# Moving evacuations between ScalarE and VectorE, and two weight gathers behind a gate, in the opening of a fused FNet-mixing and channel-mix kernel

## The chip, the cores and the metric

The kernel runs on one core of one Trainium2 chip. The metric is the device time of one execution in microseconds, the median over several runs. The core has TensorE (PE, matrix products into PSUM), VectorE (DVE), ScalarE (ACT) and GpSimd (POOL), each with its own instruction queue that is worked off in order, and 16 DMA engines. SyncE (SP) issues DMAs only.

## The reference

The input x has 8 batches of 3072 positions by 256 features. First it is mixed by a Fourier transform over both axes, of which the real part is kept; then a channel-mix layer follows, with a shift by one position:

```python
X = np.fft.fft(x, axis=1)
X = np.fft.fft(X, axis=2)
x = X.real
x_prev = np.concatenate([np.zeros((B, 1, D)), x[:, :-1, :]], axis=1)
xk = mu_k * x + (1.0 - mu_k) * x_prev
xr = mu_r * x + (1.0 - mu_r) * x_prev
k = np.maximum(xk @ w_k, 0.0)            # w_k: 256 x 1024
v = k * k @ w_v                          # w_v: 1024 x 256
r = 1.0 / (1.0 + np.exp(-(xr @ w_r)))    # w_r: 256 x 256, "receptance"
out = r * v
```

## The kernel before

**The stages of one batch.** x is loaded and folded with its mirror image by VectorE (`fold`, L171 and L173). A first set of products (`a_sum`, L583, or `a_item` and `a_half`) with a table of sines gives `a`; a second (`d_units`, L605) gives `g_all`; `turned` (L628) puts one column in another order; a third (`c_sums`, L647) gives the mixed sequence `y` as 27 slots of 128 columns per half. From `y`, VectorE forms the difference of neighbouring slots (`diff`, L700), scales it by mu (L712) and adds it (L723), which gives the two operands x for `w_k` and `w_r`. The channel mix works on 48 chunks of 512 positions: products with `w_k` (`k_products`, L758), Relu on ScalarE (L779), square on VectorE or ScalarE (`square`, L789 and L787), products with `w_v` (`v_part`, L822, in the first chunks, `v_tile`, L810, later), products with `w_r` and a sigmoid (`r_item`, L796 and L801), and the product of both (`v_out`, L832), which is stored.

**How the order is set.** Each chunk has four steps; a table of (step, function) pairs written out by hand tells what else is issued in each step: the transforms of later batches, their loads, the mixing. At the end `pin_order` chains all the instructions of an engine in the order in which they were written, so the source order is the order of every queue. The first batch has no earlier work to hide behind. It runs in an opening stretch of some 23 us, written out line by line (L844 to L969), in which TensorE also gets matmuls on zeros (`keep_busy`, L206) that compute nothing.

**PSUM.** Products go to three slots of 128x1024 (`ps_w`) and two of 128x512 (`ps_v`), each used in turn; a product has to wait until the slot's former content has been copied out. The copy out is `evac` (L518): by VectorE if its last argument is "V", otherwise by ScalarE. Two engines that use the same PSUM tile are put one after the other.

**The angles.** The table `m_cs` for the third set of products is the sine of `ang`, an integer tile with two planes (c = 0 and 1) of 14 columns of 64. The first 6 columns come from VectorE (`m_angles`, L411), the other 8 from ScalarE (`m_angles_2`, L405), one operation of 128x512 out of PSUM for each plane. VectorE then masks them to one turn (`wrap_angles`, L402; 128x768 for the first 6 columns, 128x1024 for the other 8), and ScalarE takes the sines (`m_sine`, L442).

**The loads of the weights.** GpSimd issues them in `loads` (L452): two gathers of rows of `w_k`, a memset, the load of all of `w_v` into `wv_sb` (L456), two gathers of rows of `w_r` (L457 and L458), and then `half_rows` (L492), an iota and a comparison that make the table `order`, which TensorE uses in `half_tables` (L497, step 3). A gather is issued at L140. `w_r`'s first reader is `r_item` in step 5 (L977).

**The gate.** GpSimd's queue runs ahead of the others. To hold a load back, `load_gate` (L464) has VectorE write a 1x1 tile and GpSimd write it after that; the loads behind it in GpSimd's queue thus start no earlier than VectorE comes to that point:

```python
def load_gate():
    V.memset(gate, 0)
    iota(gate, pattern=[[0, 1]], base=0, channel_multiplier=0)
```

Its first use is `loads_1` in step 1 (L974), ahead of the loads of the second batch.

**The end of the opening** (L892 to L922). The slots 0 to 4 of `y` are in the tile `first`, 5 to 8 in `w`, 9 to 16 in the two small tiles `odd` (9, 11, 13, 15) and `even` (10, 12, 14, 16). L905 makes the first four slots of x straight from `first`. Then `y` is evacuated: 5 to 8 by ScalarE (L919), slot 4, 128x128, by ScalarE (L920), the odd ones, 128x512, by VectorE and the even ones by ScalarE (L921 and L922). After that come the first products with `w_k` (`k_early`, L961), the difference of slots 4 to 8 (L962) and the rest of the steps.

Of the kernel before, what the change touches and what calls it, by code (L numbers as in the profile page):

```python
# [13 lines left out]
AF = mybir.ActivationFunctionType  # L14
# [6 lines left out]
def _v(ap, extra_offset, free_dims):  # L21
    new_ap = [list(ap.ap[0])] + [[s, c] for (s, c) in free_dims]
    return dataclasses.replace(ap, offset=ap.offset + extra_offset, ap=new_ap)
# [16 lines left out]
def kernel(  # L40
# [10 lines left out]
    nc = tc.nc  # L51

    B, S, D = x.shape
# [24 lines left out]
    def ps_w():  # L78
        return ps_slot("W", 3, 1024)

    def ps_v():
        return ps_slot("V", 2, 512)
# [23 lines left out]
    V = nc.vector  # L106
# [32 lines left out]
    def gather(dst, src, idx):  # L139
        nc.gpsimd.indirect_dma_start(dst, None, src, bass.IndirectOffsetOnAxis(ap=idx, axis=0))  # L140
# [47 lines left out]
    wr_sb = [[const.tile([P, 256], FP16, name=f"wr{m}{a}") for a in range(2)] for m in range(2)]  # L188
# [10 lines left out]
    TURN = 1 << 22  # L199
# [50 lines left out]
    row_i = const.tile([P, 4], UINT32)  # L250
# [24 lines left out]
    def ts(out, in0, s1, op0, s2=None, op1=None):  # L275
        kw = {} if op1 is None else {"op1": op1}
        V.tensor_scalar(out=out, in0=in0, scalar1=s1, scalar2=s2, op0=op0, **kw)

    MUL, ADD = ALU.mult, ALU.add
# [47 lines left out]
    for i in range(2):  # L327
        nc.scalar.activation(out=unit[:, i:i + 1], in_=g_i[0:2], func=AF.Copy, bias=1.0 - i,
                             scale=2.0 * i - 1.0)
# [19 lines left out]
    def row(n, k=1):  # L349
# [11 lines left out]
    ph_c = const.tile([P, 4], FP32)  # L361
    ang = (k2_pool.tile([P, 8, 512], FP16, name="rl", tag="rl")
           .rearrange("p a b -> p (a b)").bitcast(INT32)[:, 0:2 * NJ * 64]
           .rearrange("p (c s t) -> p c s t", c=2, t=64))
# [20 lines left out]
    for c in range(2):  # L385
        nc.scalar.activation(out=tv(TO, 32 * c, (64, 2), (1, 32)),
                             in_=_v(one, 32 * c, [(64, 2), (1, 32)]), func=AF.Copy,
                             bias=32.0 - 64.0 * c)
# [6 lines left out]
    for g in range(2):  # L395
        kw = dict(func=AF.Sin, bias=sc[:, 2 + g:3 + g], scale=sc[:, g:g + 1])
        nc.scalar.activation(out=_v(w_pm, g, [(WA + WB, 2), (2, 2), (4, NU)]),
                             in_=_v(u_w, 0, [(0, 2), (NU, 2), (1, NU)]), **kw)
        nc.scalar.activation(out=_v(w_pm, WA + g, [(WA + WB, 2), (2, NU)]),
                             in_=_v(u_w, 2 * NU, [(0, 2), (1, NU)]), **kw)  # L400
# [2 lines left out]
        ts(ang[:, :, j0:j1], ang[:, :, j0:j1], TURN - 1, ALU.bitwise_and)  # L403

    def m_angles_2(ps, j0, j1):  # L405
        for c in range(2):
            nc.scalar.activation(out=ang[:, c, j0:j1], in_=ps[:, 0:64 * (j1 - j0)],
                                 func=AF.Identity, bias=ph_c[:, 2 * c:2 * c + 1],
                                 scale=float(TURN) / S)

    def m_angles(ps, j0, j1, z=0):  # L411
        for c in range(2):
# [36 lines left out]
    def m_first():  # L449
        nc.gpsimd.memset(_v(m_cs[hi64], 0, [(NJ * 64, 2)]), 0.0)  # L450

    def loads():  # L452
        for a in range(2):
            gather(wk_sb[0][a], moe_w_k, row_i[:, a:a + 1])
        m_first()
        nc.gpsimd.dma_start(out=wv_sb, in_=moe_w_v.rearrange("(fc p) v -> p fc v", p=128))  # L456
        for a in range(2):  # L457
            gather(wr_sb[0][a], moe_w_r, row_i[:, a:a + 1])  # L458
        half_rows()


# [2 lines left out]
    def load_gate():  # L464
        V.memset(gate, 0)  # L465
        iota(gate, pattern=[[0, 1]], base=0, channel_multiplier=0)  # L466

    def loads_1():
        load_gate()
        load_xh(1, 0)  # L470
# [21 lines left out]
    def half_rows():  # L492
        iota(order_i, pattern=[[1, 2], [2, 64]], base=0, channel_multiplier=-1)
        nc.gpsimd.tensor_scalar(out=order, in0=order_i, scalar1=0.0, scalar2=None,
                                op0=ALU.is_equal)
# [22 lines left out]
    def evac(out_ap, in_ap, eng):  # L518
        if eng == "V":
            V.tensor_copy(out=out_ap, in_=in_ap)  # L520
        else:
            nc.scalar.activation(out=out_ap, in_=in_ap, func=AF.Copy)  # L522
# [86 lines left out]
    def d_evac(ps, u0, n, bank, eng):  # L609
        evac(_v(g_all, 256 * u0, [(64, 2), (128, 2 * n), (1, 64)]),  # L610
             _v(ps, 0, [(bank, 2), (64, 2 * n), (1, 64)]), eng)
# [47 lines left out]
    def y_evac(b, s0, n, ps):  # L659
        o = s0 % 2  # L660
        evac(y_t[b][:, s0:s0 + n].rearrange("p s a t -> p (s a t)"),
             _v(ps, 512 * o, [(128, n // 2), (512 - 1024 * o, 2), (1, 128)]), "A")
# [180 lines left out]

    mu_rows()  # L844
    m_angles_2(ang_ps[1], NJ1, NJ)
    wrap_angles(NJ1, NJ)
    ts(w_pm[:, 0:2, WA:WA + WB], w_pm[:, 0:2, WA:WA + WB], math.sqrt(0.5), MUL)
# [16 lines left out]
    a_sum(0, 0, 4)  # L864
    V.tensor_copy(out=muf_t, in_=mu_ps[:, 0:6])
    loads()
    keep_busy(NF[2], ang_ps[1])
    fold(0, 1, 0, 4)
# [16 lines left out]
    w, first = ps_w(), ps_w()  # L885
# [8 lines left out]
    turned(2, 4, small[1][:, 256:258], "V")  # L894
    d_evac(fill[:, 256:1024], 4, 1, 512, "A")
    d_evac(fill[:, 384:1024], 5, 1, 512, "V")
    x_t[0, 0, 0] = mix_pool.tile([P, 2, 1536], FP16, name="x00")
    for a in range(2):
        t = x_t["t", a] = mix_pool.tile([P, 24, 64], FP16, name=f"t{a}")
        nc.scalar.activation(out=t[:, 0:4],  # L900
                             in_=_v(first, 64 * a, [(128, 2), (512, 2), (1, 64)]), func=AF.Copy,
                             scale=mu_n[:, a, 0:1])
# [7 lines left out]
    y, odd = y_t[0], ps_v()  # L910
# [6 lines left out]
    keep_busy(NF[6], w[:, 768:1024], 256)  # L917
    c_sums((even, odd), 9, 8, 1)
    y_evac(0, 5, 4, w)  # L919
    evac(y[:, 4].rearrange("p a t -> p (a t)"), first[:, 256:384], "A")  # L920
    for z, p in enumerate((odd, even)):  # L921
        evac(_v(y, 128 * (9 + z), [(256, 4), (1, 128)]), p, "VA"[z])  # L922

# [93 lines left out]
    at(21, mix, 1, 0, 0, 1, 0, 12)  # L1019
    at(22, diff, 1, 12, 26)  # L1020
    at(21, load_gate)
    at(21, load_xh, 3, 1)
    at(23, mix, 1, 0, 0, 0, 12, 24)
# [18 lines left out]
    for b in range(B):  # L1042
# [4 lines left out]
        if b and b + 3 < B:  # L1047
            at(s0 + 22, load_gate)
            for h in range(2):
                at(s0 + 22, load_xh, b + 3, h)  # L1050
        t = b + 2
        if t < B:
# [6 lines left out]
            c = [(c_pairs, t, 8 * n, (8, 8, 8, 4)[n], EV[n]) for n in range(4)]  # L1059
# [7 lines left out]
        t = b + 1  # L1067
# [67 lines left out]
```

## Time and profile before

| | us |
|---|---|
| median of 3 runs | 432.34 |
| lowest and highest run | 432.31, 433.6 |
| profiled execution, its own time | 431.6 |
| its span in the profile | 429.8 |
| TensorE busy, of the span | 422.8 |
| VectorE busy | 359.8 |
| ScalarE busy | 321.6 |
| GpSimd busy | 63.9 |

The span runs from the first to the last instruction in the trace; the profiled execution's own time has 1.8 us more around it. A row of the time line gives the start and the length in us, the engine (PEld is TensorE's load of weights), the line in the kernel, the operation, and what it writes and reads; "xN" stands for N instructions merged into one row, and the bracket tells how long the engine had been idle and what ended that. A row of the chain gives start, length and what. A row of the stretches gives the stretch, its length, busy time and number of instructions of PE, PEld, DVE, ACT and POOL, the clock granted to TensorE, the DMA share and the GB/s. "DMA to landing" counts from the start of the issue to the last byte.

### The profile page before, as it was taken

The numbers are of one execution on the slowest core, as the hardware profiler recorded it, in microseconds if no ns is written. First come the engines' busy times: TensorE is split into PE (matmuls) and PEld (weight loads), VectorE is DVE, ScalarE is ACT, GpSimd is POOL, SyncE is SP. The second block draws the span as 40 slices with busy tenths as digits, with TensorE's granted clock in tenths as the row PEclk, the third lists the DMA queues.
The fourth block names the chain that finished last, engine by engine and source line by source line (L and its number), as shares of the span: only waits on it lengthen the run. The fifth ranks groups of instructions, "written<-read, shape, count | busy, mean of one in ns | idle before, by whom it ended". The sixth has DMA issues, their size and how long they took to land.

```text
span 429.8 us, 9299 instructions
## 1 busy us (share of the span) xinstructions
PE 422.8 (98%) x3858; PEld 298.5 (69%) x3858; DVE 359.8 (84%) x545; ACT 321.6 (75%) x376; POOL 63.9 (15%) x94
## 2 busy tenths in 40 slices
PE   8999999999999999999999999999999999999996
PEld 3667776777777776776677777777767767766765
DVE  8889989997998889988898988989799847997453
ACT  8889897877878678776777777777786867666661
POOL 7568402000050002300041000500000000000000
PEclk9999999999999999999999999999999999999999
DMA  8879946322385233933258223773232322223233
GB/s 173 113 117 195 229 116 130 75 56 68 70 153 143 52 77 65 197 83 72 57 116 187 57 54 73 133 159 75 52 72 50 76 65 60 69 64 72 67 73 99
DMA packets 35102, 42.06 MB, mean 98 GB/s; under 512 B 4114, under 2 KB 31092, under 8 KB 35060
## 3 DMA queue, kind: packets, MB, share of 16 engines
q1 hardware_dynamic: 27488, 25.41, 23.9%
q0 software_dynamic: 7264, 15.80, 22.0%
q8 instruction: 30, 0.49, 0.5%
q10 hardware_dynamic: 308, 0.26, 0.2%
q14 instruction: 12, 0.10, 0.1%
HBM read 32.08 MB, written 25.17 MB: 133 GB/s over the span
## 4 chain that ended last, share of the span: by engine, by line
PE 93%; POOL 2%; DMA 2%; issue 0%; DVE 0%; ACT 0%
PE psW L758 38%; PE psV L810 36%; PE psW L796 10%; PE psV L822 3%; PE psW L605 2%; DMA wv_sb<-in_moe_w_v_dram 2%; PE psW L679 1%; PE psW L565 1%; POOL xm L140 1%; PE psW L647 1%; POOL wk L140 1%; PE psW L583 0%; ACT rl L779 0%; POOL row_i L242 0%; PE psW L542 0%
## 5 line engine op out<-in xcount | busy, mean ns | idle before, releaser
L779 ACT ACTIVATE rl<-psW 128x1024 f16<-128x1024 f32 x192 | 195.2, 1025 | 92.2 <-PE psW L758 88.6
L758 PE MATMUL psW<-x,wk 128*128 128x512 f16 (+1 forms) x776 | 195.3, 377 | 0.6 <-DVE x L723 0.4
L810 PE MATMUL psV<-wv_sb,k 128*128 128x256 f16 x1424 | 184.1, 273 | 0.0
L810 PEld LDWEIGHTS <-k 128*128 128x128 f16 x1424 | 137.0, 98 | 35.7
L789 DVE TENSOR_TENSOR k<-rl 128x2048 f16<-128x2048 f16 (+1 forms) x100 | 115.6, 1157 | 33.7 <-ACT rl L779 33.3
L758 PEld LDWEIGHTS <-wk 128*128 128x128 f16 x776 | 74.8, 98 | 53.2 <-issue 1.1
L832 DVE SCALAR_TENSOR_TENSOR o<-psV,r 128x512 f32<-128x512 f32 (+1 forms) x97 | 65.8, 681 | 14.8 <-PE psV L810 13.4
L723 DVE TENSOR_TENSOR x<-y,t 128x1536 f16<-128x1536 f16 (+3 forms) x74 | 62.1, 845 | 2.1
L796 PE MATMUL psW<-wr,x 128*128 128x256 f16 x384 | 49.8, 273 | 0.0
L801 ACT ACTIVATE r<-psW 128x1024 f16<-128x1024 f32 x48 | 48.9, 1018 | 0.8 <-PE psW L796 0.8
L796 PEld LDWEIGHTS <-x 128*128 128x128 f16 x384 | 37.5, 98 | 14.3 <-issue 0.2
L466 POOL IOTA gate<- 1x1 int32 x6 | 2.1, 356 | 202.4 <-DVE gate L465 202.4
L522 ACT ACTIVATE a<-psW 128x832 f16<-128x832 f32 x31 | 25.9, 863 | 1.4 <-PE psW L565 1.4
L522 ACT ACTIVATE g_all<-psW 128x1024 f16<-128x1024 f32 (+5 forms) x37 | 25.6, 693 | 0.4 <-PE psW L628 0.2
L140 POOL DMA_INDIRECT xm<-in_x_dram,idx_g x18 | 22.9, 1271 | 5.5 <-issue 5.2
L171 DVE TENSOR_TENSOR p<-xp,xm 112x2304 f16<-112x2304 f16 (+6 forms) x19 | 21.6, 1138 | 0.0
L712 DVE TENSOR_SCALAR t<-d,muf_t 128x1536 f16<-128x1536 f16 (+3 forms) x42 | 21.2, 518 | 0.1
L712 DVE TENSOR_SCALAR t<-d,mu_m 128x1536 f16<-128x1536 f16 x32 | 19.7, 616 | 0.0
L605 PEld LDWEIGHTS <-a 128*128 128x128 f16 x208 | 14.0, 98 | 6.8 <-ACT a L522 0.7
L182 DVE TENSOR_TENSOR eo<-p 112x1152 f16<-112x1152 f16 (+3 forms) x28 | 17.9, 679 | 0.0
L700 DVE TENSOR_TENSOR d<-y 128x1664 f16<-128x1664 f16 (+5 forms) x19 | 16.7, 881 | 0.7 <-ACT y L522 0.7
L522 ACT ACTIVATE pq<-psW 128x1024 f16<-128x1024 f32 (+1 forms) x18 | 15.2, 880 | 2.3 <-PE psW L679 2.3
(137 smaller groups left out, 219.6 us busy)
## 6 DMA issues: line engine op xcount, KB each, us to landing
out_dram<-o SPq DMA_DIRECT2D x189, 128.0 KB, 2.4
xp<-in_x_dram POOLq DMA_DIRECT2D x12, 216.0 KB, 4.5
xp<-in_x_dram POOLq DMA_DIRECT2D x13, 192.0 KB, 6.9
xp<-in_x_dram POOLq DMA_DIRECT2D x2, 384.0 KB, 6.6
wv_sb<-in_moe_w_v_dram POOLq DMA_DIRECT2D x1, 512.0 KB, 9.6
xp<-in_x_dram SPq DMA_DIRECT2D x1, 480.0 KB, 4.0
xp<-in_x_dram POOLq DMA_DIRECT2D x1, 432.0 KB, 4.8
xm<-in_x_dram,idx_g POOLq DMA_INDIRECT x18, 7.8
```

The costliest lines, as they stand in the source:

```text
L140: nc.gpsimd.indirect_dma_start(dst, None, src, bass.IndirectOffsetOnAxis(ap=idx, axis=0))
L522: nc.scalar.activation(out=out_ap, in_=in_ap, func=AF.Copy)
L605: nc.tensor.matmul(out=ps[:, o:o + 128], lhsT=a_t[b][:, e, 2 * (u0 + i):2 * (u0 + i) + 2, :], rhs=w_eo[:, e], start=True, stop=True)
L712: V.tensor_scalar(out=dst, in0=src, scalar1=mu, scalar2=None, op0=ALU.mult)
L723: V.tensor_tensor(out=_v(x_t[b, j, m], o, [(64 * step, hi - lo), (step, 64)]), in0=y_t[b][:, lo + 3 * m:hi + 3 * m, a], in1=x_t["t", a][:, ...
L758: nc.tensor.matmul(out=st["k", ds][:, 512 * hs + lo:512 * hs + hi], lhsT=wk_sb[m][a][:, 128 * fc:128 * fc + 128], rhs=xk[:, a, 512 * i + l ...
L779: nc.scalar.activation(out=st["rl"][:, 2 * ds:2 * ds + 2], in_=st["k", ds].rearrange("p (f t) -> p f t", f=2), func=AF.Relu, bias=0.0, sca ...
L789: V.tensor_tensor(out=k2_t[c][:, lo:hi], in0=r, in1=r, op=ALU.mult)
L796: nc.tensor.matmul(out=ps[:, 256 * tb:256 * tb + 256], lhsT=x_t[b, 1, m][:, a, 512 * i + 128 * tb: 512 * i + 128 * tb + 128], rhs=wr_sb[m] ...
L801: nc.scalar.activation(out=st["r", c], in_=ps, func=AF.Sigmoid)
L810: nc.tensor.matmul(out=st["v", tb - h][:, 256 * h:256 * h + 256], lhsT=k2_t[c][:, fc, 128 * tb:128 * tb + 128], rhs=wv_sb[:, fc], start=(f ...
L832: V.scalar_tensor_tensor(out=o.rearrange("p a b -> p (a b)")[:, 0:256 * n], in0=st["v", t0][:, 0:256 * n], scalar=16.0, in1=st["r", c][:, ...
```

## The change

Three edits, all in the opening. First, the angles of the second plane, which ScalarE made, are made by VectorE. Second, slot 4 of `y` is copied out by VectorE in place of ScalarE, and the odd slots 9 to 15 by ScalarE in place of VectorE. Third, the two gathers of `w_r` leave `loads` and come in a new function `loads_0`, behind a gate of their own, which is called just ahead of the tile x00; `half_rows` thereby moves up behind the load of `w_v`.

```diff
     def m_angles_2(ps, j0, j1):
-        for c in range(2):
-            nc.scalar.activation(out=ang[:, c, j0:j1], in_=ps[:, 0:64 * (j1 - j0)],
-                                 func=AF.Identity, bias=ph_c[:, 2 * c:2 * c + 1],
-                                 scale=float(TURN) / S)
+        nc.scalar.activation(out=ang[:, 0, j0:j1], in_=ps[:, 0:64 * (j1 - j0)],
+                             func=AF.Identity, bias=ph_c[:, 0:1], scale=float(TURN) / S)
+        ts(ang[:, 1, j0:j1], ps[:, 0:64 * (j1 - j0)], float(TURN) / S, MUL, ph_c[:, 2:3], ADD)
...
         nc.gpsimd.dma_start(out=wv_sb, in_=moe_w_v.rearrange("(fc p) v -> p fc v", p=128))
-        for a in range(2):
-            gather(wr_sb[0][a], moe_w_r, row_i[:, a:a + 1])
         half_rows()
...
+    def loads_0():
+        load_gate()
+        for a in range(2):
+            gather(wr_sb[0][a], moe_w_r, row_i[:, a:a + 1])
+
     def loads_1():
         load_gate()
...
     d_evac(fill[:, 384:1024], 5, 1, 512, "V")
+    loads_0()
     x_t[0, 0, 0] = mix_pool.tile([P, 2, 1536], FP16, name="x00")
...
     y_evac(0, 5, 4, w)
-    evac(y[:, 4].rearrange("p a t -> p (a t)"), first[:, 256:384], "A")
+    evac(y[:, 4].rearrange("p a t -> p (a t)"), first[:, 256:384], "V")
     for z, p in enumerate((odd, even)):
-        evac(_v(y, 128 * (9 + z), [(256, 4), (1, 128)]), p, "VA"[z])
+        evac(_v(y, 128 * (9 + z), [(256, 4), (1, 128)]), p, "A")
```

## The prediction, on record before the change was run

> **What bounds the kernel now.** I read the page first, then the chain that ended last, then TensorE's own rows in the stretch that the change touches.
>
> ```profile
> span 429.8 us, 9299 instructions
> ...
> PE 422.8 (98%) x3858; PEld 298.5 (69%) x3858; DVE 359.8 (84%) x545; ACT 321.6 (75%) x376; POOL 63.9 (15%) x94
> ```
>
> TensorE is busy for 422.8 of 429.8 us. Only 7.0 us of the span are not matmul, so a change to other engines can gain something only where one of those 7.0 us lies, or lose by adding to them. The chain (columns: start, length, what) says where TensorE takes over:
>
> ```profile
> 13.76 9.57 DMA wv_sb<-in_moe_w_v_dram
> 23.38 1.03 PE psV L822 x8
> ...
> 421.23 4.51 PE psV L810 x40
> ```
>
> From 23.38 to 421.23 + 4.51 = 425.74 the chain is in effect TensorE's program order, 402.4 us. Before 23.38 its last link is no engine: it is the load of wv_sb, issued at 13.76 and landed at 13.76 + 9.57 = 23.33. Now TensorE just before it:
>
> ```profile
> 20.10 1.03 PE L758 MATMUL psW<-x,wk 128*128 128x256 f16 x8 [0.44 <-DVE x L723]
> 20.97 0.28 PE L605 MATMUL psV<-w_eo,a 128*128 128x128 f16 x2
> 21.08 1.97 PE L758 MATMUL psW<-x,wk 128*128 128x512 f16 x8
> 23.38 0.81 PE L822 MATMUL psV<-wv_sb,k 128*128 128x256 f16 x6 [0.33 <-DMA wv_sb<-in_moe_w_v_dram]
> ```
>
> TensorE waits twice in this stretch: 0.44 us at 20.10 for the mixed x of VectorE, 0.33 us at 23.38 for wv_sb. The reader is to see their order. Whatever is saved at the first is paid back at the second, as long as wv_sb still lands at 23.33. So every part is judged by one question: when does the first L822 matmul start?
>
> **Part 1, the angle operation.** VectorE's rows, then ScalarE's:
>
> ```profile
> 6.08 0.54 DVE L277 TENSOR_SCALAR rl<-psV,ph_c 128x320 int32<-128x320 f32 x1
> 6.65 0.59 DVE L277 TENSOR_SCALAR rl<-rl 128x768 int32<-128x768 int32 x1
> 7.72 0.69 DVE L277 TENSOR_SCALAR rl<-rl 128x1024 int32<-128x1024 int32 x1 [0.48 <-ACT rl L407]
> ```
> ```profile
> 6.45 1.23 ACT L407 ACTIVATE rl<-psV,ph_c 128x512 int32<-128x512 f32 x2
> ```
>
> Removed: one of ScalarE's two, 1.23 / 2 = 0.61 us, so ScalarE is free near 7.07 instead of 7.68. Added on VectorE: the same operation on 128x512. It isn't in the trace; the nearest row is 128x320 at 0.54, so it lies between 0.54 and 0.54 x 512 / 320 = 0.86. I take 0.70, the middle, which is also about the 0.68 of a 128x512 copy out of PSUM (quoted below). In the changed instruction order it waits for ScalarE's half, which reads the same PSUM tile, but that ends near 7.07, before VectorE is through with the first mask at 6.65 + 0.59 = 7.24. So it runs 7.24 to 7.94 and the second mask starts there instead of at 7.72: VectorE had 0.48 us of idle time, uses it up and is 0.2 late (by the ends, 0.06 to 0.4). The folds of x stand behind it on VectorE and shift by 0.2. ScalarE, on the other side, reaches the sines and the table load up to 0.6 earlier. What becomes of both is read where they meet:
>
> ```profile
> 13.93 0.56 ACT L522 ACTIVATE a<-psV 128x416 f16<-128x416 f32 x1
> ```
> ```profile
> 14.54 0.40 PE L605 MATMUL psV<-w_eo,a 128*128 128x128 f16 x4 [0.23 <-ACT a L522]
> ```
>
> The next TensorE stage waits for the last evacuation of a. That one reads the product of the last fold, so it follows VectorE, and a ScalarE that is free sooner doesn't help it. I cost Part 1 at 0.1 us later at 14.54 (ends 0 and 0.4), hidden further on by the wait at 23.38.
>
> **Part 2, the evacuations of the sums.** VectorE, then ScalarE:
>
> ```profile
> 17.27 1.13 DVE L905 SCALAR_TENSOR_TENSOR x<-psW,muf_t,t 128x128 f16<-128x128 f32 x4 [0.33 <-ACT t L900]
> 18.32 0.68 DVE L520 CAST y<-psV 128x512 f16<-128x512 f32 x1
> 18.91 0.42 DVE L700 TENSOR_TENSOR d<-y 128x512 f16<-128x512 f16 x1
> ```
> ```profile
> 18.43 0.28 ACT L522 ACTIVATE y<-psW 128x128 f16<-128x128 f32 x1 [0.31 <-DVE x L905]
> 18.61 0.59 ACT L522 ACTIVATE y<-psV 128x512 f16<-128x512 f32 x1
> 19.09 0.60 ACT L522 ACTIVATE y<-psW 128x512 f16<-128x512 f32 x1
> 19.56 1.11 ACT L522 ACTIVATE g_all<-psV 128x512 f16<-128x512 f32 x2
> 20.95 1.02 ACT L779 ACTIVATE rl<-psW 128x1024 f16<-128x1024 f32 x1 [0.28 <-PE psW L758]
> ```
>
> VectorE gives away the 128x512 copy (it held the queue 18.91 - 18.32 = 0.59) and takes a 128x128 one; a 128x128 operation of L905 costs 1.13 / 4 = 0.28. So the difference at 18.91, the mixed x behind it and TensorE's matmuls at 20.10 come 0.59 - 0.28 = 0.3 earlier, inside the 0.44 waited there. ScalarE loses its 0.31 of waiting and the 128x128 copy, which moved its queue by 18.61 - 18.43 = 0.18, and gains a 128x512 copy at 19.09 - 18.61 = 0.48 of queue: 0.48 - 0.18 - 0.31 puts the two g_all copies where they were, or 0.1 later with the handover from TensorE. They end by 19.56 + 1.11 + 0.1 = 20.77, so the first L779 starts near 20.8 instead of 20.95. The square that L822 needs comes next on VectorE:
>
> ```profile
> 22.42 1.30 DVE L789 TENSOR_TENSOR k<-rl 128x1024 f16<-128x1024 f16 x2
> ```
>
> With VectorE 0.3 earlier and L779 ending near 21.8, it starts near 22.1 and ends after 1.30 / 2 = 0.65 at 22.8. TensorE's second half of 21.08, which reuses a PSUM slot that L779 frees, ends 0.15 to 0.3 before its 23.05. So without the wait for wv_sb, L822 could start near 22.95: about 0.45 is the most that Parts 1 and 2 can give, and with wv_sb at 23.33 they give nothing.
>
> **Part 3, the gathers of w_r behind a gate.** On GpSimd the two gathers stood between the wv_sb load and the two operations that make the order table; now those two come first, then the gate, then the gathers.
>
> ```profile
> 13.76 1.21 POOL L456 DMA_DIRECT2D wv_sb<-in_moe_w_v_dram  x1
> 15.27 0.98 POOL L140 DMA_INDIRECT wr<-in_moe_w_r_dram,row_i  x1 [0.30 <-issue]
> 16.56 0.94 POOL L140 DMA_INDIRECT wr<-in_moe_w_r_dram,row_i  x1 [0.30 <-issue]
> ```
> ```profile
> 16.53 0.42 DVE L520 CAST g_all<-psW 128x256 f16<-128x256 f32 x1
> ```
>
> The gate is one VectorE memset behind that copy, at 16.95, in the 0.33 of idle time before 17.27, so it costs VectorE nothing. GpSimd's iota waits for it, and what is queued behind that wait are the two gathers and, behind them, the next gate of before, which starts only at 23.20:
>
> ```profile
> 23.20 0.12 POOL L466 IOTA gate<- 1x1 int32 x1 [4.76 <-DVE gate L465]
> ```
>
> From that row, the memset (23.05) leads to the iota 0.15 later, and the next issue follows 0.23 behind it: the gathers issue at 16.95 + 0.15 + 0.23 = 17.3 and 17.3 + 0.98 + 0.30 = 18.6, 2.0 later than now, and GpSimd is done at 19.6, well ahead of 23.2. Nothing else moves. The load of wv_sb keeps its issue at 13.76, since nothing that precedes it on GpSimd was edited. Does it land earlier without the gathers close behind? The landing times of the two gathers, first and second (min/median/max over one and over two issues):
>
> ```profile
> DMA to landing us min/median/max: 8.4/8.4/8.4
> ```
> ```profile
> DMA to landing us min/median/max: 7.4/7.9/8.4
> ```
>
> They land at 15.27 + 8.4 = 23.67 and 16.56 + 7.4 = 23.96, that is 0.34 and 0.63 after wv_sb, in the order of issue. And the transfers end in a tail that a few engines make (last two columns: DMA share, GB/s):
>
> ```profile
> 21.00:22.00 1.00, 1.00 (x8) 0.47 (x6) 1.00 (x4) 1.00 (x2) 0.00 (x0) 1.00 0.34 46
> 22.00:23.00 1.00, 1.00 (x5) 0.29 (x3) 1.00 (x3) 1.00 (x2) 0.00 (x0) 1.00 0.22 29
> ```
>
> Two thirds of the DMA capacity lie idle while the last packets of wv_sb come in, so those few engines aren't short of bandwidth. They work off a queue in which the gathers stand behind. I read this as no gain for wv_sb; the bounds are 0 and the two gathers' whole share, 0.63, of which TensorE could use 0.45. The Trainium skill (DMA: Bandwidth & Descriptors, section "Two DMAs through the same engine are not ordered") says that descriptors of one queue of one SDMA engine start in order but are pipelined, which speaks against this part: by it the gathers behind can't hold up wv_sb's start, and only the pipelining leaves a little; the order of landing agrees.
>
> Sum: 0 for Part 1 and 2 (behind the wait for wv_sb), 0 for Part 3, against the profiled execution's 431.6 us. That lies 0.74 under the median of 432.34, so I forecast the median itself, rounded: **432.3 us**.
>
> **The rivals.**
> *A, forecast: wv_sb still lands near 23.3.* 432.3 us. The wait at 20.10 shrinks to 0.1 or 0.2 and the one at 23.38 grows by as much.
> *B, wv_sb lands earlier.* If the gathers' packets were interleaved with wv_sb's, it lands up to 0.63 sooner and L822 gains up to 0.45, less the 0.1 of Part 1: 0.35, so 432.0 us. For it: the gathers finish only 0.34 and 0.63 behind wv_sb, which is short for 256 rows on a queue. Against it: the order of landing, the idle capacity.
> *C, w_r is late (slower).* Its first reader:
>
> ```profile
> 27.69 1.04 PE L796 MATMUL psW<-wr,x 128*128 128x256 f16 x8
> ```
>
> The second gather, issued at 18.6, must land within 27.69 - 18.6 = 9.1 us. The rows show 7.4 and 8.4, but the slowest gather of the first 60 us needed 11.5:
>
> ```profile
> DMA to landing us min/median/max: 3.2/6.3/11.5
> ```
>
> At 11.5 it lands at 30.1, and TensorE, in order, stands for 2.4 us: 434.7 us. Below 9.1 it costs nothing. Against it: the queue ahead is empty by 24, and the next load is issued only at 23.4.
> *D, a GpSimd issue ahead of wv_sb stretches.* VectorE's shift of 0.2 changes what runs beside the gathers before 13.76. One issue can take twice its usual 0.98:
>
> ```profile
> 34.22 1.93 POOL L140 DMA_INDIRECT wr<-in_moe_w_r_dram,row_i  x1 [0.30 <-issue]
> ```
>
> That would put wv_sb 1.93 - 0.98 = 0.95 later: 433.3 us. The Trainium skill (SBUF — State Buffer, section "Who interferes with whom") has the mechanism: VectorE in a 2-port mode and GpSimd exclude each other from shared ports for a whole instruction. No row here proves that this is what stretched that issue.
>
> **How the numbers follow.** About 0.3%, 1.3 us, is what a measurement of this kernel can tell from no change. A 0.48, B 0.26, D 0.10: all three within it. C 0.12: mostly slower, since a stall of over 1.3 us needs a landing past 10.4 us. What no row prices: 0.04 faster. Faster 0.04, same 0.85, slower 0.11. The range takes in A, B and D, 0.84 together: from 432.3 less 0.45 and some scatter, 431.6, to 433.3.
>
> **What would show it.** Part 1: the second mask 0.1 to 0.3 later, the first evacuation of a earlier, L605 still at 14.5 to 14.7. Part 2: L700 near 18.6, the L758 group at 19.8. Part 3: the two gathers issued near 17.3 and 18.6, and L796 without a wait. The forecast itself: L822 starts at 23.3 to 23.4 and the wait for wv_sb there is 0.6 to 0.8. It is wrong if L822 starts under 23.2 (B), if wv_sb's issue is off 13.76 (D), or if L796 waits for w_r (C).

## The result, and the profile after

| | median, us | lowest to highest, us | runs |
|---|---|---|---|
| before, in the first comparison | 432.37 | 432.26 to 433.63 | 8 |
| changed, in the first comparison | 431.61 | 431.44 to 431.94 | 8 |
| before, beside e5, e6, e7 and e8 | 431.44 | 431.20 to 432.33, and one of 489.85 | 33 |
| changed, e5 | 431.65 | 431.32 to 431.98 | 11 |
| before, beside e13 to e16 | 431.43 | 431.19 to 432.31 | 33 |
| changed, e16 | 431.45 | 431.35 to 431.96 | 11 |

The first comparison gave a ratio of 0.9973 (95 % interval 0.9961 to 0.9986): faster by 0.76 us. Two later ones gave 1.0003 (0.9994 to 1.0012) and 1.0001 (0.9992 to 1.0010). The changed kernel took the same each time. What varied is the kernel before, which ran 0.7 to 0.9 us slower in the first comparison than in the later ones. So two things need an explanation: what can slow the kernel before, and why it doesn't slow the changed one.

The page of the changed kernel's profiled execution (431.82 us):

```profile
span 430.0 us, 9302 instructions
...
PE 423.8 (99%) x3858; PEld 299.0 (70%) x3858; DVE 360.3 (84%) x547; ACT 321.5 (75%) x375; POOL 62.9 (15%) x95
```

TensorE's rows at the end of the opening (L760 and L824 are L758 and L822 of before):

```profile
20.42 1.03 PE L760 MATMUL psW<-x,wk 128*128 128x256 f16 x8
21.29 0.28 PE L607 MATMUL psV<-w_eo,a 128*128 128x128 f16 x2
21.41 2.19 PE L760 MATMUL psW<-x,wk 128*128 128x512 f16 x8
23.49 1.05 PE L824 MATMUL psV<-wv_sb,k 128*128 128x256 f16 x8
```

The wait for wv_sb is gone, but TensorE reaches the products with w_v at 23.49, no sooner than the 23.38 of before. GpSimd's queue is what looks different. First the changed kernel, then the one before:

```profile
7.44 0.65 POOL L242 IOTA row_i<- 64x2 uint32 x4
...
8.50 0.93 POOL L140 DMA_INDIRECT xm<-in_x_dram,idx  x1
9.73 1.20 POOL L140 DMA_INDIRECT wk<-in_moe_w_k_dram,row_i  x1 [0.30 <-issue]
11.23 1.35 POOL L140 DMA_INDIRECT wk<-in_moe_w_k_dram,row_i  x1 [0.30 <-issue]
...
12.67 0.95 POOL L455 DMA_DIRECT2D wv_sb<-in_moe_w_v_dram  x1
```
```profile
7.44 1.20 POOL L242 IOTA row_i<- 64x2 uint32 x4
...
9.04 1.64 POOL L140 DMA_INDIRECT xm<-in_x_dram,idx  x1 [0.16 <-issue]
10.99 1.37 POOL L140 DMA_INDIRECT wk<-in_moe_w_k_dram,row_i  x1 [0.30 <-issue]
12.67 1.01 POOL L140 DMA_INDIRECT wk<-in_moe_w_k_dram,row_i  x1 [0.30 <-issue]
```

No line of this part of GpSimd's queue was edited. Still the gathers of w_k issue 1.26 and 1.44 us sooner, and the load of w_v at 12.67 instead of 13.76. VectorE's rows of the same stretch, the changed kernel and then the one before, show why:

```profile
7.16 0.73 DVE L277 TENSOR_SCALAR rl<-psV,ph_c 128x512 int32<-128x512 f32 x1
7.93 0.71 DVE L277 TENSOR_SCALAR rl<-rl 128x1024 int32<-128x1024 int32 x1
...
8.88 1.22 DVE L171 TENSOR_TENSOR p<-xp,xm 96x1024 f16<-96x1024 f32 x1
```
```profile
8.66 1.21 DVE L171 TENSOR_TENSOR p<-xp,xm 96x1024 f16<-96x1024 f32 x1
9.91 0.17 DVE L173 TENSOR_TENSOR p<-xp,xm 96x4 f16<-96x4 f32 x1
9.99 0.68 DVE L171 TENSOR_TENSOR p<-xp,xm 96x1024 f16<-96x1024 f16 x1
```

Before, the mask at 7.72 (in the prediction's fence) fell into the four iotas, which took 1.20 instead of 0.65. So the gather of xm started at 9.04, after the first fold at 8.66, and ended at 10.68, when the second fold ended (9.99 + 0.68 = 10.67). In the changed kernel the angle operation puts the mask at 7.93, behind these four iotas. It now falls on the two small iotas after them, which take 0.53 and 0.46 instead of 0.12 each, but that costs less: the gather starts at 8.50, ahead of the fold at 8.88, and takes 0.93. A shift of 0.2 us on VectorE thus became 1.1 to 1.4 us on GpSimd.

Of the loads in this queue, the one with the least room is not w_v but w_k. Before, the second gather of w_k was issued at 12.67 and needed

```profile
DMA to landing us min/median/max: 5.3/5.3/5.3
```

so it landed at 17.97, while the first products with w_k start at 18.04:

```profile
18.04 1.05 PE L758 MATMUL psW<-x,wk 128*128 128x256 f16 x8
```

The second four of these eight read it, half of 1.05 us later, near 18.5. The kernel before had 0.5 us to spare; in its second profile (e1 below) the gather landed at 12.04 + 6.2 = 18.24, only 0.2 us ahead of the same point, near 18.45. In the changed kernel the gather was issued at 11.23 and, with the 5.0 us measured for it in e5, landed at 16.2, more than 2 us ahead.

### The profile page after: what moved, and what is told of

Its sections match the earlier page's. It is cut to its first block, busy times and chain, and to the rows that moved or that the text cites. A ratio compares the mean times of both kernels' runs of the same rounds, so it can differ in the third digit from the quotient of the medians.

```text
span 430.0 us, 9302 instructions
## 1 busy us (share of the span) xinstructions
PE 423.8 (99%) x3858; PEld 299.0 (70%) x3858; DVE 360.3 (84%) x547; ACT 321.5 (75%) x375; POOL 62.9 (15%) x95
## 4 chain that ended last, share of the span: by engine, by line
PE 97%; ACT 1%; DVE 1%; issue 0%; POOL 0%
PE psW L760 38%; PE psV L812 36%; PE psW L798 10%; PE psV L824 3%; PE psW L607 2%; PE psW L681 1%; PE psW L567 1%; PE psW L206 1%; PE psW L585 1%; PE psW L649 1%; PE psV L347 1%; ACT rl L781 0%; ACT y L524 0%; PE psV L649 0%; ACT g_all L524 0%; PE psV L585 0%
## 5 line engine op out<-in xcount | busy, mean ns | idle before, releaser
L760 PE MATMUL psW<-x,wk 128*128 128x512 f16 (+1 forms) x776 | 195.4, 377 | 0.3
L760 PEld LDWEIGHTS <-wk 128*128 128x128 f16 x776 | 74.9, 98 | 53.0 <-issue 0.7
```

The costliest lines, as they stand in the source:

```text
L760: nc.tensor.matmul(out=st["k", ds][:, 512 * hs + lo:512 * hs + hi], lhsT=wk_sb[m][a][:, 128 * fc:128 * fc + 128], rhs=xk[:, a, 512 * i + l ...
```

## The experiments

Three theories were held against each other. *GpSimd's queue*: what is gained is that w_k and w_v issue sooner. *The queue of the DMA engines*: the gathers of w_r, moved away, let w_v land sooner. *Evacuations*: the shorter chain on VectorE is what counts. The interval of a ratio is some 0.001 either way, so single parts of 0.2 us are read from the traces rather than from the times.

**e1, the kernel before again.** No edit.

> The kernel before, unchanged, for a second profile. Its profiled execution took 431.6 us with the first L822 matmul at 23.38, while its eight runs lie at 432.3 or 433.6. If the first profile was a lucky one and the load of w_v sets the end of the opening in the usual run too, a second profile shows a time near 432.3 or 433.6 with L822 at 24.1 or 25.4 and a wait for wv_sb of 1 us or more there. If the spread has another source (the clock of TensorE, the tail of the run), L822 stays near 23.4 and the difference lies elsewhere. Time: ratio 1.000 within 0.003.

431.63 us beside 431.63, ratio 0.9999 (0.9990 to 1.0008). The profiled execution took 431.36, L822 started at 23.05 and there was no wait for wv_sb: issued at 13.36, it needed 8.9 us and landed at 22.26. A median near 432.4 us for the kernel before did not come back in any of the later comparisons.

**e2, e3 and e4: Part 1, Part 3 and Part 2 alone.** Each is one of the three edits of the diff above.

> Part 1 alone: the angle operation on VectorE, evacuations and gathers as before. Theory GpSimd (the masks on VectorE move away from GpSimd's iotas, so the load of w_v is issued at 12.7 instead of 13.8 and lands some 1 us sooner): 431.5 to 431.9, most of the gain, and in the trace L456 issues near 12.7. Theory queue (the gathers of w_r behind w_v hold it up): no gain, 432.3. Theory evacuations (the VectorE chain before the first squares set the end): no gain or 0.1 slower.

> Part 3 alone: the two gathers of w_r behind the gate, all else as before. Theory GpSimd: L455 still issues near 13.8, 432.3, no gain. Theory queue: w_v lands 0.3 to 1.0 sooner with its issue where it was, 431.4 to 432.0. Theory evacuations: 432.3.

> Part 2 alone: slot 4 on VectorE, the odd slots on ScalarE. Theory GpSimd and theory queue: no gain, 432.3, since the wait for wv_sb takes up the 0.3 us; in the trace the L758 group starts near 19.8 and the wait for wv_sb is the longer by as much. Theory evacuations: 0.3 to 0.7 faster, 431.6 to 432.0.

Ratios 0.9993 (0.9984 to 1.0002), 1.0003 (0.9994 to 1.0012) and 0.9991 (0.9982 to 1.0000), all beside 431.63 us. None has the 0.76 us; in e1's profile TensorE had no wait for a load that they could have removed. The traces answer more. With Part 1 alone the load of w_v issues at 12.66; with Part 3 alone at 13.89, with Part 2 alone at 13.41. That is what GpSimd's theory says of the issue. For the DMA queue, w_v without the gathers behind it (e3) landed at 13.89 + 8.3 = 22.19, hardly sooner than 22.26 in e1. Against the 23.33 of the very first profile it is 1.1 us sooner, but so is e1 without any edit, and in neither did TensorE wait for w_v. A gain of the size of the 0.63 in the prediction is therefore not seen; a small one can't be excluded. For Part 2, I take the stretch from the first L605 of the time line to the first product with w_v, in e1, in e4 and in the full change (e5):

```profile
14.43 0.40 PE L605 MATMUL psV<-w_eo,a 128*128 128x128 f16 x4
...
23.05 1.05 PE L822 MATMUL psV<-wv_sb,k 128*128 128x256 f16 x8
```
```profile
15.10 0.40 PE L605 MATMUL psV<-w_eo,a 128*128 128x128 f16 x4
...
23.52 1.05 PE L822 MATMUL psV<-wv_sb,k 128*128 128x256 f16 x8
```
```profile
14.89 0.40 PE L607 MATMUL psV<-w_eo,a 128*128 128x128 f16 x4
...
23.47 1.05 PE L824 MATMUL psV<-wv_sb,k 128*128 128x256 f16 x8
```

8.62, 8.42 and 8.58 us: Part 2 saves 0.20, and the full change has given 0.16 of it back. With Part 3 alone the stretch is 8.62, as in e1.

**e5 and e6: the changed kernel again, and Parts 1 and 2 without Part 3.**

> The changed kernel again, beside the kernel before. The first comparison gave 0.9973, with the kernel before at 432.3 or 433.6; where the single parts were run, the kernel before took 431.6 (33 runs, 431.25 to 432.22) and none of the parts gained 0.1 %. If the gain belongs to the change as a whole, the ratio is again near 0.997. If it was the kernel before that was slow in that first comparison, the changed kernel takes 431.4 to 431.9 again and the ratio is whatever the kernel before does: 0.999 to 1.000 with it at 431.6, 0.997 with it at 432.4.

> Parts 1 and 2 without the gathers. Part 1 alone took the issue of the load of w_v from 13.4 - 13.9 to 12.7 and Part 2 alone ran at 431.28. If both are needed together (an early w_v and a short VectorE chain), 431.0 to 431.2, and L822 before 22.9. If the start of the products with w_v is set by something else by now (ScalarE's chain, the clock of TensorE in the opening), 431.3 to 431.6.

e5: 431.65 beside 431.44, ratio 1.0003 (0.9994 to 1.0012). e6: 431.17, ratio 0.9996 (0.9986 to 1.0005), with L821 at 23.70 - 15.28 = 8.42 behind its first L604, as with Part 2 alone. So Part 3, on top of Part 2, is what costs the 0.16. The row that shows it, in the changed kernel's first profile, is the scaling of the difference, beside the second gather of w_r (19.04 to 19.99):

```profile
19.53 0.58 DVE L714 TENSOR_SCALAR t<-d,muf_t 128x256 f16<-128x256 f16 x2
```

It took 0.48 before. In e8 below, where the same gather ran beside the same operations, the gather took 1.16 instead of 0.95, the scaling 0.48, and the stretch 8.41: one or the other is longer. That the two overlap is not enough: with Part 3 alone (e3) the scaling ran at 19.78, beside a gather from 19.09 to 20.04, and neither was longer than usual. What decides it is not shown.

**e7 and e8: w_v issued late, in both kernels.** Nothing is left out; GpSimd has eight iotas more.

```diff
+        for _ in range(8):
+            iota(pause, pattern=[[1, P]], base=0, channel_multiplier=0)
         nc.gpsimd.dma_start(out=wv_sb, ...)
```

> The kernel before with eight iotas to a tile of their own ahead of the load of w_v on GpSimd, about 2 us; nothing is left out. In the second profile of the kernel before, w_v landed at 22.3 and L822 began at 23.05, so there is 0.8 us of room. If w_v is what can make the kernel before slow, this one is 1.0 to 1.5 us slower (ratio 1.0025 to 1.0035), with a wait for wv_sb of that size ahead of L822: the size of the first comparison's gap. If w_v doesn't matter, ratio 1.000.

> The changed kernel with the same eight iotas ahead of the load of w_v. There the load is issued 0.7 to 1.2 us sooner, so of the 2 us some 1.2 to 2.0 fall into the room before L822: 0 to 0.5 us slower than the changed kernel, 431.6 to 432.1, clearly faster than the kernel before with the same delay. If the changed kernel has no more room than the one before, it is 1.0 to 1.5 us slower as well.

Both missed. e7: 431.79, ratio 1.0007 (0.9997 to 1.0016), L825 at 23.63 with no wait for wv_sb. Issued at 16.55 instead of 13.36, w_v landed at 16.55 + 6.0 = 22.55 instead of 22.26. e8: 431.21, ratio 0.9997 (0.9988 to 1.0006); there w_v, issued at 15.30 instead of 12.66, landed at 21.10, against 12.66 + 8.5 = 21.16 in e16, the same kernel without the iotas. So within these pairs the issue hardly moved the landing; that the loads ahead of it set the landing is my inference. A late issue of w_v does not make a gap of 0.7 to 0.9 us, and I turned to all the loads at once.

**e9 to e12: one more load of 512 KB, in four kernels.** It goes to a tile that nobody reads; the result is the same.

```diff
         nc.gpsimd.memset(_v(m_cs[hi64], 0, [(NJ * 64, 2)]), 0.0)
+        nc.gpsimd.memset(extra[:, 0:1], 0.0)
+        nc.sync.dma_start(out=extra, in_=x[7, 0:1024].rearrange("(p a) d -> p (a d)", p=128)[:, 0:1024])
```

> The kernel before with one more load, 512 KB of x to a tile that nothing reads, issued by SyncE just ahead of the load of w_v: it makes the DMA engines slower for everybody, as they might be where the kernel before took 432.3 or 433.6 us. If late transfers are what slowed it there, w_v lands 1.5 to 2.6 us later (512 KB at some 200 GB/s), L822 waits for it 1 to 2 us and the time is 432.4 to 433.7. If transfers have nothing to do with it, below 0.4 us slower than the kernel before without the load.

> The changed kernel with the same extra load. If it is what it does under slow transfers that made the first comparison, it gains 0.7 to 1.7 us on the kernel before with the same load: 431.4 to 432.3. If both suffer alike, the first comparison has another source that this doesn't show.

> Part 1 alone with the extra load. Theory GpSimd: w_v issues 0.7 to 1.2 us sooner, so this has most of the changed kernel's gain over the kernel before with the load. Theory queue: none of it.

> Part 3 alone with the extra load. Theory queue: the two gathers are out of w_v's way, w_v lands 0.6 us or more sooner than in the kernel before with the load and the time falls by as much. Theory GpSimd: no gain, or up to 0.2 slower from the gathers beside VectorE's chain.

Medians, beside 431.50 us for the kernel before without the load: before with the load (e9) 432.20, the changed kernel (e10) 431.36, Part 1 alone (e11) 431.68, Part 3 alone (e12) 432.13. Ratios: 1.0010 (1.0001 to 1.0019), 1.0001 (0.9992 to 1.0009), 1.0002 (0.9993 to 1.0010), 1.0022 (1.0004 to 1.0040). By the medians the changed kernel is 0.84 us ahead of the one before, near the 0.76 of the first comparison; by the ratios it is 0.4 us, and their intervals overlap. Of eleven runs each, nine take over 431.8 us in e9 and four in e10. The runs of e12 go up to 436.21. TensorE in e9, then GpSimd, then the landing of both gathers of w_k:

```profile
17.85 0.61 PE L761 MATMUL psW<-x,wk 128*128 128x256 f16 x4
20.20 0.61 PE L761 MATMUL psW<-x,wk 128*128 128x256 f16 x4 [1.74 <-DMA wk<-in_moe_w_k_dram,row_i]
...
24.36 0.38 PE L825 MATMUL psV<-wv_sb,k 128*128 128x256 f16 x2 [0.22 <-DMA wv_sb<-in_moe_w_v_dram]
```
```profile
12.48 1.09 POOL L140 DMA_INDIRECT wk<-in_moe_w_k_dram,row_i  x1 [0.30 <-issue]
```
```profile
DMA to landing us min/median/max: 4.1/5.9/7.7
```

The second gather, issued at 12.48, needs 7.7 us and lands at 20.18; TensorE has done the first four products and stands for 1.74 us. In e10 it issues 1.24 us sooner and lands in time:

```profile
11.24 1.34 POOL L140 DMA_INDIRECT wk<-in_moe_w_k_dram,row_i  x1 [0.30 <-issue]
```
```profile
DMA to landing us min/median/max: 5.3/5.3/5.3
```

11.24 + 5.3 = 16.54, and the eight products run at 18.03 without a wait. The extra load is issued when GpSimd has issued w_k, so it comes behind both gathers in either kernel (at 13.9 in e9, 12.9 in e10). Why the same gather needs 7.7 us in one and 5.3 in the other is not shown; the profiles with the load are set side by side below. In e12 the same four products waited 1.44 us; the bracket names x, but the gather landed at 12.66 + 7.8 = 20.46, just ahead of their start at 20.51. In e11, Part 1 alone, they didn't wait. The wait was expected at w_v (1 to 2 us at L822); it came at w_k, and 0.22 us of it at w_v.

**e13 and e14: GpSimd sooner, with VectorE and ScalarE as before.**

```diff
-    rows()
     load_m0(0)
+    rows()
```

> The kernel before with two lines of GpSimd's queue exchanged: the gather of the first row of x (load_m0) ahead of the six iotas of row_i instead of behind them; VectorE and ScalarE as before. In the profiles so far that gather took 0.93 us where it started ahead of VectorE's first fold (8.50 against 8.88) and 1.47 to 1.64 where it started behind it (9.04 against 8.66). Here it starts near 7.6, so by the theory of GpSimd's queue it takes 0.93 and the gathers of w_k issue 0.5 to 1.2 us sooner without any change to the angles. Time: 431.4 to 431.6, within 0.001 of the kernel before, since there is no wait for transfers to remove where those arrive in time.

> The same exchange with the extra load of 512 KB. The kernel before took 432.2 with that load and waited 1.7 us for w_k, the changed one 431.36 and didn't wait. Theory of GpSimd's queue: the exchange alone brings most of it back, 431.3 to 431.8, and the wait for w_k is gone or below 0.5. If the changed kernel owed its robustness to the balance of VectorE and ScalarE, 432.0 to 432.4.

e13: 431.38 beside 431.43, ratio 1.0001 (0.9992 to 1.0010). e14, with the load: 431.54, ratio 1.0000 (0.9991 to 1.0009), against 432.20 in e9, and TensorE doesn't wait for w_k. GpSimd in e14:

```profile
8.06 1.12 POOL L140 DMA_INDIRECT xm<-in_x_dram,idx  x1 [0.59 <-POOL idx L264]
9.20 0.69 POOL L243 IOTA row_i<- 64x2 uint32 x4
...
10.30 1.23 POOL L140 DMA_INDIRECT wk<-in_moe_w_k_dram,row_i  x1 [0.16 <-issue]
11.83 1.32 POOL L140 DMA_INDIRECT wk<-in_moe_w_k_dram,row_i  x1 [0.30 <-issue]
```

Nothing of the change is in this kernel. Two lines exchanged on GpSimd do what the change does under load: one run of eleven takes over 431.8 us, against nine in e9.

**e15 and e16: Parts 1 and 2 with the load, and the changed kernel once more.**

> Parts 1 and 2 with the extra load. Part 2 shortened the stretch from the first L605 to L822 by 0.2 us in the profiles, Part 3 gave 0.16 back. Theory of GpSimd's queue: 431.1 to 431.4, no slower than the changed kernel with the load (431.36), since the gathers of w_r have no share in it. Theory queue of the DMA engines: slower than the changed kernel by 0.3 us or more.

> The changed kernel once more, for what the kernel before does beside it. Where it runs at 431.4 to 431.6, ratio 0.999 to 1.0005; where it runs at 432.3 or 433.6 as in the first comparison, ratio 0.996 to 0.998, with the changed kernel at 431.4 to 431.9 in either case.

e16: 431.45 beside 431.43, ratio 1.0001 (0.9992 to 1.0010). e15 missed: 431.71, from 431.20 to 432.93, ratio 1.0007 (0.9998 to 1.0016). Its profile (432.16 us) has GpSimd in the late order (the gather of xm behind the first fold) although Part 1 is in, and a wait for w_k:

```profile
9.05 1.65 POOL L140 DMA_INDIRECT xm<-in_x_dram,idx  x1 [0.16 <-issue]
```
```profile
19.98 0.61 PE L760 MATMUL psW<-x,wk 128*128 128x256 f16 x4 [1.52 <-DMA wk<-in_moe_w_k_dram,row_i]
```

In this execution VectorE ran 0.2 us ahead of the changed kernel's profile (mask at 7.73 instead of 7.93), so the iotas were caught again. The gather of xm took 1.47 us or more in all seven profiles without Part 1 and without the exchange, and 0.93 or 0.94 in all five of the changed kernel (with e8 and e10); Part 1 without Part 3 gave early order twice (e2, e6) and late order twice (e11, e15). Part 1 moves the odds, it doesn't fix the order. Whether Part 3 has a share in that can't be told from five profiles. The exchange fixed it in all four of its profiles (0.93 to 1.13).

**e17 and e18: the exchange with Part 2**, without and with the load.

> The exchange on GpSimd (load_m0 ahead of the iotas of row_i) with Part 2, angles and gathers of w_r as before: the two things that the runs show to be worth something, without the rest. Part 2 alone gave 431.28 beside 431.63, the exchange alone 431.38 beside 431.43. Expected 431.1 to 431.25, ratio 0.9992 to 0.9997 of the kernel before; from the first L605 to L822 8.4 us as in the profile of Part 2 alone, and w_k issued by 12. If the two don't add up, 431.3 to 431.5.

> The same with the extra load of 512 KB. Theory of GpSimd's queue: no wait for w_k, 431.2 to 431.5, against 432.2 for the kernel before with the load and 431.36 for the changed one. If Part 2 exposes w_k again by its shorter chain, a wait for it of up to 0.5 us and 431.5 to 432.

e17: 431.28 beside 431.44, ratio 0.9997 (0.9988 to 1.0006), from L605 to L822 22.97 - 14.55 = 8.42. e18: 431.68, ratio 1.0001 (0.9992 to 1.0010), no wait for w_k and 0.41 for wv_sb. Both medians are above what was expected, and in e18 the wait that came is the one for w_v, not for w_k. The version has the shorter chain, and no wait for w_k under the load; by the times it beats neither kernel by more than the interval.

**All profiles side by side.** The seven with the extra load:

| run | second gather of w_k issued | from issue to landing, us | extra load issued | wait of TensorE for w_k, us |
|---|---|---|---|---|
| e10 | 11.24 | 5.3 | 12.9 | none |
| e14 | 11.83 | 6.0 | 13.5 | none |
| e18 | 11.84 | 5.5 | 13.5 | none |
| e11 | 12.27 | 5.3 | 13.9 | none |
| e9 | 12.48 | 7.7 | 13.9 | 1.74 |
| e12 | 12.66 | 7.8 | 14.0 | 1.44 |
| e15 | 12.68 | 7.3 | 14.1 | 1.52 |

All the waits are where the gather issued last. But e11 has GpSimd in the late order, with w_v issued at 14.00 as in e9, and still no wait: an early queue on GpSimd was enough in these profiles, but not needed in e11. Where there was a wait, the extra load also followed the gather more closely (1.3 to 1.4 us instead of 1.6 to 1.7). Which of the two makes the landing late is not shown.

The stretch from the first L605 to the first product with w_v, where no wait for a load or the gate lies in it, is 8.62 or 8.63 us in all six profiles without Part 2, 8.41 or 8.42 in e4, e6, e8 and e17, and 8.58 in the other four of the changed kernel. Without the extra load, e4, e6, e8 and e17 also have the lowest medians, 431.17 to 431.28; all others lie at 431.38 to 431.79, the first comparison's kernel before apart. No single one of these differences is clear of its interval, but they agree with the traces.

## Why the prediction was wrong, point by point

- **The forecast, "the median itself", no change:** wrong in the comparison it was made for (0.9973). That the two later ones show no change is not to its credit: the mechanism behind it, A, was not what happened. The wait at 23.38 did not grow, it vanished, and the kernel before didn't have it either in e1. Nor did its range hold by a mechanism: 431.61 lies below the 431.85 that the largest priced gain gives, in the part that was put down to scatter.
- **The step that failed** is in Part 3, which the sum put at 0: "The load of wv_sb keeps its issue at 13.76, since nothing that precedes it on GpSimd was edited." It moved to 12.67 (12.66 in e5 and e16), and the two gathers of w_k ahead of it by 1.26 and 1.44 us. The instructions were the same, their lengths were not. I had the mechanism in rival D, with the row (1.93 against 0.98), but priced it only as a loss of 0.95; the 1.64 us of the gather at 9.04 showed that before had already paid, so a gain was as open. Whether this step accounts for the 0.76 us is a second question, and stays open (below).
- **The wrong resource.** I asked when w_v lands and not when w_k does. The row at 12.67 and its landing, 0.5 us ahead of its use, were to be had.
- **The spread of the runs.** 432.31 beside 433.6, and a profiled execution 0.74 below the median, were signs of a kernel before that sometimes waits for something its profile doesn't show. I added the 0.74 back as a constant, as if the changed kernel had to have it too. It was the size of the effect: the changed kernel took 431.61, and the kernel before itself 431.43 to 431.63 in all later comparisons.
- **Part 1:** the second mask 0.2 later, right; L605 at 14.5 to 14.7, right where TensorE's opening ran alike (14.54 in e16), 14.91 in the first profile for a reason given below. Its effect through GpSimd was missed.
- **Part 2:** 0.3 expected at the difference, 0.20 measured from L605 to L822; right in kind. The term that was too small is the 128x128 copy, put at 0.28: it held VectorE's queue for 19.07 - 18.68 = 0.39 us in the changed kernel. Inside the wait for w_v it should have given nothing; there was mostly no such wait (e1).
- **Part 3:** the gate and the gathers' times came as worked out relative to the first L605. "No gain for w_v" was not contradicted (e3), but one of its reasons doesn't hold: a DMA share of 0.34 or 0.22 is a mean over 16 engines and doesn't tell whether the few still at work were full. That the gathers would cost VectorE nothing is wrong by 0.16 together with Part 2, and right without it (e3).
- **Rival C:** w_r was never waited for.

What stays open is the cause of the 0.76 us: none of the runs at 432.3 or 433.6 was profiled. That they waited for w_k under slower transfers is inferred from e9 and e10, whose medians are nearly as far apart, and is not shown. One thing speaks against it: the eight runs of the first comparison lie in two narrow groups, 432.26 to 432.39 and 433.60 to 433.63, while those of e9 are spread from 431.43 to 432.79 and none reaches the second group. Some other condition of that first comparison could as well be behind it; it did not come back on either of the two chips of the later runs (e5 to e8 ran on one, the others on another).

## What to carry to other kernels

An edit on VectorE can move GpSimd's DMA issues although no line of GpSimd is touched; look in the profile at the start and length of each gather beside VectorE's rows, and price the shift in both directions. For each load, set its landing against its first use, not only for the one that the chain shows: a margin of 0.2 to 0.5 us doesn't show as a wait and is the first to go when transfers are slower. Where the runs of the kernel before scatter by more than the effect at stake, or the profiled one lies outside them, find out what varies first.

## What the runs showed of the hardware that I had not expected

- **VectorE and GpSimd take turns.** In these rows a gather that starts behind a fold ends when a later fold ends (10.68 and 10.67 us; in the changed kernel 12.58 and 11.88 + 0.68 = 12.56), and the gather of xm takes 0.93 to 1.13 where it starts ahead of the first fold. In e4 the gather at 10.99 took 0.95 and the fold that started beside it at 10.95 took 0.76 instead of 0.68. The Trainium skill (SBUF — State Buffer, section "Who interferes with whom") says that the order of issue, not the shape, decides who blocks; the rows of xm's gather agree. The row of e4 does not clearly: there the fold started 0.04 us first, and it is the one that was longer.
- **TensorE's first matmuls differ from run to run.** The eight matmuls on zeros, first in e1 and then in e5:

```profile
5.81 1.90 PE L206 MATMUL psW<-zeros 128*128 128x512 f16 x8
```
```profile
6.07 3.37 PE L206 MATMUL psW<-zeros 128*128 128x512 f16 x8
```

  Over all profiles they took 1.89 to 3.56 us, while the four that follow took 1.04 in each. The first L605 came at 14.35 to 15.28, and the long ones among them go with a late L605: 14.85 to 15.10 in the six from 3.32 us on. The latest, 15.28 (e6), has another source: VectorE waited 0.56 us for a load of x. The granted clock in the profile's rows reads 1.00 throughout. The Trainium skill (TensorE: Matmul & The Clock Gate, section "What's actually happening") describes a clock that rises after a busy window which runs freely and isn't reset by the kernel's start; the spread agrees with that, and no row here shows the window itself.
- **A late issue needn't land late.** w_v issued 3.2 us later (e7 against e1) landed 0.3 us later, and 2.6 us later (e8 against e16) landed no later at all.
